# A second chunk of every fourth head computed twice, and the first loads, low parts and products reordered

## The chip, the cores and the metric

The kernel runs on one core of a Trainium2 chip. Its engines are TensorE (PE in the profile; PEld is its weight load), VectorE (DVE), ScalarE (ACT), GpSimd (POOL) and SyncE (SP), which here issues all transfers between HBM and the on-chip memory. The metric is the device time of one execution in microseconds, median of several runs; lower is better. Matrix products write to PSUM, which has eight banks of 128 x 512 numbers.

## The reference

Two independent results for S = 2048 tokens of width D = 448 are written side by side.

```python
# part A: Fourier mixing, written as products with given matrices
a = einsum("bsd,ed->bse", x, dft_hid_re)
b = einsum("bsd,ed->bse", x, dft_hid_im)
y = einsum("ts,bse->bte", dft_seq_re, a) - einsum("ts,bse->bte", dft_seq_im, b)
# part B: full attention with H = 16 heads of 28
q, k, v = split(x @ wqkv)
scores = einsum("bhqd,bhkd->bhqk", q, k) * 28 ** -0.5
o = einsum("bhqk,bhkd->bhqd", softmax(scores), v)
out = concatenate([y, o @ wo], axis=-1)
```

## The kernel before

**Numbers.** A product of 32-bit numbers is made of products of a coarser type (float32r): an operand is split in a high part, which ScalarE's copy makes, and a low part, which is the operand less its high part (a subtraction). Width 448 is three blocks of 128 and one of 64, whose high and low parts share one block; so a product over 448 is a chain of 11 matrix products into one bank: high by high, low by high and high by low for three blocks, and two for the last.

**Stages.** `load_x` brings the input of part B in four chunks of 512 tokens, four blocks each, and splits it. `project(j, w, chunks)` makes block j of q and k (seven blocks of 128 rows), one chain of width 512 a chunk; ScalarE and VectorE copy its high and low part out, and both are stored to HBM (`qkd`), from where each head's rows are read again (`k`, `qk`, `qr`). `values` makes V, one chain of width 448 for each 128 tokens (16 in all); VectorE's copy (L604) takes it out, and a store with rows of 128 bytes lays it out by head (`vd`). These two, and part A (`hidden`, `sequence`, L652), are "fill" work: they use two PSUM banks of their own (`NFILL = 2`), and attention has the other six. At the end the output projection (L959) follows.

**Attention** goes in 64 units (head h, chunk c of 512 queries), and each needs the maximum of a query's 2048 scores before the exponential. There are two ways:

- `unit_kept`: 16 products of scores (L793), each copied to SBUF by ScalarE (L406) and compared into a running maximum by VectorE (L803); then four transposes (L810), a reduction (L812), four transposes that spread the maximum over the partitions (L819), a subtraction over two tiles at once by GpSimd or VectorE (L836), and an exponential over two tiles at once by ScalarE (L840).
- `unit_twice`: 16 products of scores the other way round (L743) whose maxima VectorE reduces straight from PSUM (L747), one small transpose (L706), a trip of the maxima through HBM into two further rows of q, and 16 products again (L771) with the maximum already taken off, which ScalarE's exponential reads from PSUM (L775).

In both, groups of eight tiles are multiplied with V (L724), in a shape of the array that uses 32 columns. `TWICE` says which chunks of a head go the second way: chunk 1 of every head, so 16 of 64.

**Order.** Nothing is ordered by hand. Every step is a task with an engine (or a choice of engines), an assumed duration and a key (its due time); `Schedule.run` plays the kernel through when it is built and emits instructions in the order that results. Units in the two ways form two lanes, each spread evenly over the attention stage (`P_R`, `P_K`); the fill work's keys come from `fkey`, which is evenly spread after a denser start. Each engine takes its instructions strictly in the order emitted.

**The start.** `make_identity` and `N_WARM = 9` products on it come first on TensorE. Then come x's first chunk, weight blocks w_0 and w_1, the other chunks, and V's weights, as the keys in the code's last part say; `project(0, ., [0])`, `project(1, ., [0])`, three more chunks of `project(0)`, and then `values`. The first chunk's low parts are VectorE's; those of later chunks and of V's weights may go to VectorE or GpSimd (`early`). In these first chains the products are sorted so that all high by high products come first.

Of the kernel before, what the change touches and what calls it, by code (L numbers as in the profile page):

```python
# [13 lines left out]
AF = mybir.ActivationFunctionType  # L14
# [7 lines left out]
D = 448  # L22
H = 16
# [12 lines left out]
Q_YO = 2  # L36
N_WARM = 9
GV = 8

TWICE = [(1,) for h in range(H)]  # L40


def f32(ap):
    return ap.bitcast(F32)
# [9 lines left out]
FLOW, FLOW_IN = 200.0, 400.0  # L54
T_IN = 20.0
X_ROWS = 2.0
AHEAD = 0.15
# [105 lines left out]
class Schedule:  # L163
# [34 lines left out]
    def run(self):  # L198
        now, events, count = 0.0, [], 0
# [108 lines left out]
def tile_kernel(ctx, tc, xa, wre, wim, wd, xb, wqkv, wo, out):  # L308
# [90 lines left out]
    def sub(key, dst, a, b, early=False, d=1.25, **kw):  # L399

        return sch.add({"DVE": 0.67} if early == "DVE" else {"DVE": 0.8, "POOL": 1.6} if early else {"POOL": d}, key,
                       lambda e: eng[e].tensor_tensor(dst(), a(), b(), op=ALU.subtract), **kw)
# [26 lines left out]

    IN = F_QKV + 11 * M512  # L430
    HEAD = IN + F_V

    def fkey(n, d):

        f = clock[0]
        clock[0] += n * d
        if f < IN:
            return 6 + f
        if f < HEAD:
            return 6 + IN + V_PACE * (f - IN)  # L440
        at = 6 + IN + V_PACE * F_V
# [9 lines left out]
    def x_3(s):  # L451
        return big[:, 6 * S + s.start:6 * S + s.stop]
# [13 lines left out]
    def load_x(c, key):  # L466
        cols = slice(c * CH, (c + 1) * CH)
        for k in range(4):
            pair = kept_s.slot()
            raw = Half(pair, 0)  # L470
            ld = dma(key + 0.3 * k, lambda raw=raw, k=k: nc.sync.dma_start(raw.t, xb[c, :, k]), use=[pair])
            hi = (lambda k=k: x_h(k, cols)) if k < 3 else (lambda: x_3(cols))
            a = act(key + 0.3 * k, lambda raw=raw, hi=hi: nc.scalar.activation(hi(), raw.t, AF.Copy), ACT_S,
                    deps=[ld], use=[pair])
            early = "DVE" if c == 0 else True
            if k < 3:
                b = sub(key + 0.3 * k, lambda k=k: x_l(k, cols), lambda raw=raw: raw.t,
                        lambda k=k: f32(x_h(k, cols)), early, deps=[a], use=[pair])
            else:
                b = sub(key + 0.3 * k, lambda: x_3(cols)[64:], lambda raw=raw: raw.t[64:],  # L480
                        lambda: f32(x_3(cols))[64:], early, deps=[a], use=[pair])
            xb_hi[c, k], xb_ready[c, k] = a, b
# [18 lines left out]
    class Piece:  # L501


        def __init__(self, src, key, kind="c", early=False):
            self.hi, self.lo = whi.slot(), wlo.slot()
            raw = wraw.slot()
            ld = dma(key, lambda: nc.sync.dma_start(raw.t, src()), acq=[raw])
            a = act(key + 1, lambda: nc.scalar.activation(self.hi.t, raw.t, AF.Copy), ACT_S,  # L508
                    deps=[ld], acq=[self.hi], use=[raw])
# [3 lines left out]
            b = sch.add(e, key + 1.5, lambda g: eng[g].tensor_tensor(  # L513
                self.lo.t[:, :n], raw.t[:, :n], f32(self.hi.t)[:, :n], op=ALU.subtract),
                deps=[a], acq=[self.lo], use=[raw, self.hi])
            self.ready, self.hi_ready, self.lo_ready = [b], a, [b]
            if kind == "x":
                self.ready.append(sch.add({g: {"DVE": 0.3, "POOL": 0.53}[g] for g in both}, key + 1.5, lambda g: eng[g].tensor_tensor(
                    self.hi.t[64:, 3], raw.t[64:, 3], f32(self.hi.t)[64:, 3], op=ALU.subtract),
                    deps=[a], use=[raw, self.hi]))  # L520
            elif kind == "w":
                self.ready.append(sch.add({g: {"DVE": 0.3, "POOL": 0.53}[g] for g in both}, key + 1.5, lambda g: eng[g].tensor_tensor(
                    self.lo.t[:64, 3], raw.t[:64, 3], f32(self.hi.t)[:64, 3], op=ALU.subtract),
                    deps=[a, b], use=[raw, self.hi, self.lo]))
                self.ready.append(sch.add({"DVE": 0.15, "POOL": 0.25}, key + 1.5, lambda g: eng[g].memset(
                    f32(self.lo.t)[64:, 3], 0.0), deps=[b], use=[self.lo]))
                self.lo_ready = self.ready
# [23 lines left out]
    def project(j, w, chunks):  # L551

        for c in chunks:
# [3 lines left out]
            wh, wl = lambda k: (lambda: w.hi.t[:, k]), lambda k: (lambda: w.lo.t[:, k])  # L557
            first = j == 0 or j == 1 and c == 0
            if first:

                seq = [(wh(k), xh(k)) for k in range(3)] + [(wl(k), xh(k)) for k in range(3)] + [
                    (wh(k), xl(k)) for k in range(3)] + [(wh(3), x3()), (wl(3), x3())]
                parts = {i: [xb_hi[c, i]] for i in range(3)}
                parts[0] = [xb_hi[c, 0], w.hi_ready]
                parts[3] = w.lo_ready
                parts.update({6 + k: [xb_ready[c, k]] for k in range(4)})
            else:
                seq = [(b, a) for a, b in products(xh, xl, x3, wh, wl)]
                parts = {0: w.ready}
# [20 lines left out]
    def values(ready):  # L590
        for c in range(NC):
            v_done[c] = []
            for t in range(4):
# [5 lines left out]
                key = fkey(11, M448)  # L599
                end = chain(key, seq, o, D, ready, [], M448, [pair], {3 * k: [xb_ready[c, k]] for k in range(4)}, v_last)  # L600

                def put(o=o, vs=vs):
# [7 lines left out]
                    vs.t.rearrange("p (h x) -> p h x", h=H)), extra=1.0, deps=[b], use=[pair]))  # L610
        x_users.append(v_last[0])

# [392 lines left out]
```

## Time and profile before

| | us |
|---|---|
| median of 3 runs | 1189.49 (1188.24 to 1190.04) |
| the profiled execution | 1188.49 |
| its span in the profile | 1186.6 |

The profile shows one execution. Busy time is the time in which an engine had an instruction under way; matrix products overlap, so the distance between starts is what one more of them costs. A wait in the profile names the instruction that ended it. A row of the time order gives start, duration, engine, line, operation, output and inputs, how many are merged, and in brackets the idle time before and what ended it. The profile's line numbers are those of the kernel before; in the changed kernel most of these lines stand some six further down.

### The profile page before, as it was taken

The numbers are of one execution on the slowest core, as the hardware profiler recorded it, in microseconds if no ns is written. First come the engines' busy times: TensorE is split into PE (matmuls) and PEld (weight loads), VectorE is DVE, ScalarE is ACT, GpSimd is POOL, SyncE is SP. The second block draws the span as 40 slices with busy tenths as digits, with TensorE's granted clock in tenths as the row PEclk, the third lists the DMA queues.
The fourth block names the chain that finished last, engine by engine and source line by source line (L and its number), as shares of the span: only waits on it lengthen the run. The fifth ranks groups of instructions, "written<-read, shape, count | busy, mean of one in ns | idle before, by whom it ended". The sixth has DMA issues, their size and how long they took to land.

```text
span 1186.6 us, 19856 instructions
## 1 busy us (share of the span) xinstructions
PE 1162.1 (98%) x6422; PEld 812.7 (68%) x6422; DVE 912.2 (77%) x1431; ACT 1052.7 (89%) x1764; POOL 965.6 (81%) x569
## 2 busy tenths in 40 slices
PE   8899999999999999999999999999999999999998
PEld 6786666676667666676666666676667676766687
DVE  6598888888888878778878888888888786877301
ACT  5379999999999989899989999999999998999733
POOL 6067778889989879888879888879989888799953
PEclk9999999999999999999999999999999999999999
DMA  7772344421323232313232233233232423223642
GB/s 269 173 135 92 111 131 155 129 79 65 93 85 102 62 115 65 105 60 114 73 109 63 95 106 97 68 94 93 75 118 72 126 70 105 80 76 115 193 143 109
DMA packets 111192, 125.18 MB, mean 105 GB/s; under 512 B 48720, under 2 KB 62672, under 8 KB 111088
## 3 DMA queue, kind: packets, MB, share of 16 engines
q1 hardware_dynamic: 111088, 123.91, 34.6%
q8 instruction: 51, 0.84, 0.3%
q14 instruction: 53, 0.43, 0.1%
HBM read 89.98 MB, written 33.75 MB: 104 GB/s over the span
## 4 chain that ended last, share of the span: by engine, by line
PE 87%; DMA 3%; ACT 3%; DVE 3%; issue 2%; SPq 1%; POOL 0%; DVEq 0%; ACTq 0%; POOLq 0%
PE bank L652 24%; PE bank L724 19%; PE bank L793 15%; PE bank L538 11%; PE bank L771 5%; PE bank L743 5%; PE bank L959 3%; PE bank L810 2%; DVE rm L803 2%; PE bank L819 2%; ACT kept L406 1%; PE bank L854 1%; DMA sm<-kept 1%; DMA kept<-xb 1%; ACT kept L840 1%
## 5 line engine op out<-in xcount | busy, mean ns | idle before, releaser
L836 POOL TENSOR_TENSOR kept<-kept,mb 128x1024 f32<-128x1024 f32 x275 | 655.7, 2407 | 94.1 <-ACT mb L821 83.8
L803 DVE TENSOR_TENSOR rm<-bank,rm 128x512 f32<-128x512 f32 x672 | 460.7, 686 | 83.4 <-ACT kept L406 33.4
L406 ACT ACTIVATE kept<-bank 128x512 f32<-128x512 f32 (+1 forms) x717 | 410.8, 629 | 55.2 <-PE bank L793 34.1
L840 ACT ACTIVATE kept<-kept 128x1024 f32<-128x1024 f32 x374 | 392.5, 1095 | 12.7 <-POOL kept L836 9.4
L652 PE MATMUL bank<-big,whi 128*128 128x448 f32 x1024 | 324.2, 370 | 0.0
L793 PE MATMUL bank<-qk,k 84*128 84x512 f32 x768 | 290.6, 408 | 4.4 <-DVE rm L803 1.4
L513 POOL TENSOR_TENSOR wlo<-wraw,whi 128x512 fp32r<-128x512 f32 (+1 forms) x165 | 202.9, 1234 | 72.0 <-ACT whi L508 48.6
L724 PE MATMUL bank<-kept,v 128*32 128x512 f32 x1984 | 240.2, 597 | 1.1 <-ACT kept L840 1.0
L652 PEld LDWEIGHTS bank<-big,whi 128*128 128x128 f32 x1024 | 193.4, 190 | 30.3 <-issue 5.0
L652 PE MATMUL bank<-big,wlo 128*128 128x448 f32 x512 | 189.2, 370 | 0.6 <-POOL wlo L513 0.6
L793 PEld LDWEIGHTS bank<-qk,k 84*128 84x128 f32 x768 | 142.8, 189 | 65.0 <-issue 15.9
L747 DVE TENSOR_REDUCE mx<-bank 128x1 f32<-128x512 f32 x256 | 172.9, 682 | 15.1 <-PE bank L743 14.0
L775 ACT ACTIVATE kept<-bank 128x512 f32<-128x512 f32 x244 | 154.7, 638 | 9.5 <-PE bank L771 9.3
L724 PEld LDWEIGHTS bank<-kept,v 128*32 128x32 f32 x1984 | 56.3, 109 | 124.1 <-issue 113.8
L508 ACT ACTIVATE whi<-wraw 128x512 fp32r<-128x512 f32 x167 | 111.2, 668 | 18.4 <-DMA wraw<-wqkv 8.0
L836 DVE TENSOR_TENSOR kept<-kept,bank 128x1024 f32<-128x1024 f32 x99 | 119.7, 1211 | 3.2 <-ACT mb L821 2.9
L652 PEld LDWEIGHTS bank<-big,wlo 128*128 128x128 f32 x512 | 97.1, 190 | 13.8 <-POOL wlo L513 1.0
L771 PE MATMUL bank<-qr,k 86*128 86x512 f32 x256 | 104.8, 411 | 1.5 <-DVE rm L803 1.5
L743 PE MATMUL bank<-k,qr 84*128 84x512 f32 x256 | 102.5, 410 | 2.9 <-DMA qr<-qkd 1.9
L538 PE MATMUL bank<-wd,whi 128*128 128x448 f32 x256 | 80.3, 370 | 0.0
L538 PE MATMUL bank<-big,whi 128*128 128x512 f32 x196 | 69.7, 412 | 4.0 <-DVE kept L579 2.6
L812 DVE TENSOR_REDUCE nm<-bank 128x4 f32<-128x512 f32 x48 | 33.1, 690 | 51.6 <-PE bank L810 47.1
(81 smaller groups left out, 1073.1 us busy)
## 6 DMA issues: line engine op xcount, KB each, us to landing
wraw<-wre SPq DMA_DIRECT2D x64, 256.0 KB
wraw<-wim SPq DMA_DIRECT2D x64, 256.0 KB
wraw<-xa SPq DMA_DIRECT2D x32, 256.0 KB
qkd<-wd SPq DMA_DIRECT2D x30, 256.0 KB
k<-qkd SPq DMA_DIRECT2D x64, 112.0 KB
out<-kept SPq DMA_DIRECT2D x32, 224.0 KB
qkd<-kept SPq DMA_DIRECT2D x26, 256.0 KB
qk<-qkd SPq DMA_DIRECT2D x48, 112.0 KB
```

The lines of the kernel that those rows point to most:

```text
L406: nc.scalar.activation(dst, src, AF.Copy)
L513: b = sch.add(e, key + 1.5, lambda g: eng[g].tensor_tensor(self.lo.t[:, :n], raw.t[:, :n], f32(self.hi.t)[:, :n], op=ALU.subtract), deps=[ ...
L538: nc.tensor.matmul(o.t[:, :cols], w(), x(), start=(i == 0), stop=(i == n - 1))
L652: nc.tensor.matmul(o.t[:, :D], a.t[:, k, :], b[:, q * 4 + k, :], start=(q == 0 and k == 0 and j == 0), stop=(q == 3 and k == 3 and j == 2))
L724: nc.tensor.matmul(o.t[j * VW:(j + 1) * VW, :], VT[h].t[:, kt // 4, j, :], pairs[i // 2].t[:, i % 2, :], start=(kt < 4), stop=(kt >= NT - 4))
L743: m = pe(key, lambda e, o=o, kc=kc, qt=qt: nc.tensor.matmul(o.t, q.t[:KR, qt * P:(qt + 1) * P], KT[h].t[:KR, kc * CH:(kc + 1) * CH], start ...
L747: ms.append(dve(key - 20, lambda o=o, kc=kc, qt=qt: nc.vector.tensor_reduce(mx.t[:, qt, kc:kc + 1], o.t, axis=AX.X, op=ALU.max), deps=[m], ...
L771: m = pe(key, lambda e, o=o, kt=kt: nc.tensor.matmul(o.t, KT[h].t[:KR + 2, kt * P:(kt + 1) * P], q.t[:KR + 2, :], start=True, stop=True), ...
L793: m = pe(key, lambda e, o=o, kt=kt: nc.tensor.matmul(o.t, KT[h].t[:KR, kt * P:(kt + 1) * P], q.t[:KR, :], start=True, stop=True), deps=[*l ...
L803: prev = dve(key - 20, lambda o=o: nc.vector.tensor_tensor(rm.t, o.t, rm.t, op=ALU.max), deps=[m, prev], use=[rm, o], lock=[o], own=RAW)
L836: eng[e].tensor_tensor(s.t, s.t, over_pair(pm.t if e == "DVE" else mb.t), op=ALU.add)
L840: es.append(act(key, lambda s=s: nc.scalar.activation(s.t, s.t, AF.Exp, scale=SCALE), 0.96, deps=[sh], use=[s]))
```

## The change

Chunk 3 of heads 2, 6, 10 and 14 also goes the `unit_twice` way, so 20 of 64 units do. In the start, all low parts of x and of V's weights are VectorE's. w_1 is no longer loaded ahead: its load, conversion and low part take their place with the other weight blocks, on GpSimd. V's weights are asked for right after x's first chunk, and V of the first chunk is made right after its `project(0)`. The first chain takes its products in the order in which its parts come, and V's chains wait for each block of weights by itself. There are 11 warm-up products. The builder's play of the start has given start times for the engines and the transfers, and `fkey` has a shorter dense start.

```diff
-N_WARM = 9
+N_WARM = 11
-TWICE = [(1,) for h in range(H)]
+TWICE = [(1, 3) if h % 4 == 2 else (1,) for h in range(H)]
+FIRST = {"PE": 1.4, "ACT": 2.0, "DVE": 2.0, "POOL": 5.0, "SP": 0.75}
+FLOW_AT = 4.1
...
-        idle = {e: True for e in self.ENGINES}
+        idle = {e: False for e in self.ENGINES}
+        for n, e in enumerate(self.ENGINES):
+            heapq.heappush(events, (FIRST[e], 0, n - 9, "free", (e, None)))
-        landed, flow = [], 0.0
+        landed, flow = [], FLOW_AT
...
     def sub(key, dst, a, b, early=False, d=1.25, **kw):
-        return sch.add({"DVE": 0.67} if early == "DVE" else {"DVE": 0.8, "POOL": 1.6} if early else {"POOL": d}, key,
+        return sch.add({"DVE": 0.69} if early else {"POOL": d}, key,
...
-    IN = F_QKV + 11 * M512
-    HEAD = IN + F_V
+    IN = F_QKV + F_V / 4
+    HEAD = F_QKV + F_V
...
-            a = act(key + 1, lambda: nc.scalar.activation(self.hi.t, raw.t, AF.Copy), ACT_S,
+            a = act(key + (0 if early else 1), lambda: nc.scalar.activation(self.hi.t, raw.t, AF.Copy), ACT_S,
+            at = key + (0 if early else 1.5)
...
-            first = j == 0 or j == 1 and c == 0
-            if first:
-                seq = [(wh(k), xh(k)) for k in range(3)] + [(wl(k), xh(k)) for k in range(3)] + [
-                    (wh(k), xl(k)) for k in range(3)] + [(wh(3), x3()), (wl(3), x3())]
-                parts = {i: [xb_hi[c, i]] for i in range(3)}
...
+            first = j == 0
+            seq = [(b, a) for a, b in products(xh, xl, x3, wh, wl)]
+            if first and c == 0:
+                seq = [seq[i] for i in (0, 1, 3, 2, 5, 4, 6, 8, 7, 9, 10)]
+                parts = {0: [xb_hi[c, 0], w.hi_ready], 1: [xb_ready[c, 0]], 2: [xb_hi[c, 1]], 3: w.lo_ready, 5: [xb_ready[c, 1]],
+                         6: [xb_hi[c, 2]], 8: [xb_ready[c, 2]], 9: [xb_ready[c, 3]]}
+            elif first:
+                parts = {3 * k: [xb_hi[c, k]] for k in range(3)}
+                parts.update({3 * k + 1: [xb_ready[c, k]] for k in range(3)})
+                parts[9] = [xb_ready[c, 3]]
...
-        return Piece(lambda: wqkv[:, :, j * P:(j + 1) * P], (0.2, 1.2)[j] if j < 2 else key, "w", j < 2)
+        return Piece(lambda: wqkv[:, :, j * P:(j + 1) * P], 0.2 if j == 0 else key, "w", j == 0)
...
-                end = chain(key, seq, o, D, ready, [], M448, [pair], {3 * k: [xb_ready[c, k]] for k in range(4)}, v_last)
+                end = chain(key, seq, o, D, [], [], M448, [pair],
+                            {3 * k: [xb_ready[c, k], ready[k], *ready[4:][:k // 3]] for k in range(4)}, v_last)
...
-    w_0, w_1 = weights_of(0), weights_of(1)
+    w_0 = weights_of(0)
+    wv = load_w(w_first, lambda k: wqkv[:, k, 2 * D:], 1.5, early=True)
     for c in range(1, NC):
         load_x(c, 1.0 + 3 * c)
-    wv = load_w(w_first, lambda k: wqkv[:, k, 2 * D:], 12.0, early=True)
     project(0, w_0, [0])
-    project(1, w_1, [0])
+    values(wv, [0])
     project(0, w_0, [1, 2, 3])
-    values(wv)
-    project(1, w_1, [1, 2, 3])
-    for j in range(2, 7):
+    values(wv, [1, 2, 3])
+    x_users.append(v_last[0])
+    for j in range(1, 7):
         project(j, weights_of(j), range(NC))
```

More of the change, by code (lines that the diff above doesn't have):

```diff
@@ L440, in fkey @@
             return 6 + IN + V_PACE * (f - IN)
[L441 removed]
+        at = 6 + IN + V_PACE * (HEAD - IN)
         return at + (f - HEAD) * (T_FILL - at) / (F_TOTAL - HEAD)
@@ L517, in __init__ @@
             if kind == "x":
-                self.ready.append(sch.add({g: {"DVE": 0.3, "POOL": 0.53}[g] for g in both}, key + 1.5, lambda g: eng[g].tensor_tensor(
+                self.ready.append(sch.add({g: {"DVE": 0.3, "POOL": 0.53}[g] for g in both}, at, lambda g: eng[g].tensor_tensor(
                     self.hi.t[64:, 3], raw.t[64:, 3], f32(self.hi.t)[64:, 3], op=ALU.subtract),
@@ L521, in __init__ @@
             elif kind == "w":
[L522 removed]
+                self.ready.append(sch.add({g: {"DVE": 0.3, "POOL": 0.53}[g] for g in both}, at, lambda g: eng[g].tensor_tensor(
                     self.lo.t[:64, 3], raw.t[:64, 3], f32(self.hi.t)[:64, 3], op=ALU.subtract),
                     deps=[a, b], use=[raw, self.hi, self.lo]))
[L525 removed]
+                self.ready.append(sch.add({"DVE": 0.15, "POOL": 0.25}, at, lambda g: eng[g].memset(
                     f32(self.lo.t)[64:, 3], 0.0), deps=[b], use=[self.lo]))
@@ L587, in weights_of, with values @@
         key = fkey(0, 0) - 12
-        return Piece(lambda: wqkv[:, :, j * P:(j + 1) * P], (0.2, 1.2)[j] if j < 2 else key, "w", j < 2)
-    def values(ready):
-        for c in range(NC):
+        return Piece(lambda: wqkv[:, :, j * P:(j + 1) * P], 0.2 if j == 0 else key, "w", j == 0)
+    def values(ready, chunks):
+        for c in chunks:
             v_done[c] = []
```

15 lines of the change are left out of this document (5 added, 10 removed).

## The prediction, made before the changed kernel ran

> **What bounds the kernel now.** I read the page first: totals, then the chain that ended last.
>
> ```profile
> span 1186.6 us, 19856 instructions
> ...
> PE 1162.1 (98%) x6422; PEld 812.7 (68%) x6422; DVE 912.2 (77%) x1431; ACT 1052.7 (89%) x1764; POOL 965.6 (81%) x569
> ...
> PE 87%; DMA 3%; ACT 3%; DVE 3%; issue 2%; SPq 1%; POOL 0%; DVEq 0%; ACTq 0%; POOLq 0%
> ```
>
> TensorE is busy 98% of the span and is 87% of the last chain. Next, the stretches, to see where it isn't (columns: PE, PEld, DVE, ACT, POOL busy, granted clock, DMA share, GB/s):
>
> ```profile
> 0.00:32.00 32.00, 25.18 (x91) 19.50 (x92) 19.65 (x30) 17.65 (x30) 18.39 (x19) 1.00 0.77 270
> ...
> 50.00:60.00 10.00, 6.52 (x26) 5.48 (x25) 5.05 (x13) 2.74 (x6) 1.60 (x3) 0.83 0.97 197
> ...
> 80.00:1160.00 1080.00, 1069.38 (x6015) 732.87 (x6014) 852.55 (x1311) 999.88 (x1673) 920.88 (x527) 1.00 0.32 99
> 984.00:992.00 8.00, 6.52 (x28) 4.86 (x31) 3.49 (x6) 5.09 (x11) 4.46 (x3) 0.79 0.39 116
> 1160.00:1186.60 26.60, 23.05 (x113) 20.81 (x111) 3.05 (x5) 9.23 (x21) 10.42 (x15) 1.00 0.27 104
> ```
>
> PE idles 6.8 us in the first 32, 3.5 us between 50 and 60, and only 10.6 us in the 1080 us after 80. The last idle time is after its last product. So a product added in the long middle is paid in full, and what can be won lies in the start, in the hole at 50 to 60, and in those 10.6 us. The list of PE's waits says what ended them:
>
> ```profile
> PE bank L538 <- DVE kept L604: 3.5, 1, 3.5
> ...
> PE bank L771 <- DVE rm L803: 1.5, 1, 1.5
> ...
> PE bank L724 <- ACT kept L840: 1.0, 1, 1.0
> ```
>
> **The four chunks that change path.** Heads 2, 6, 10 and 14 compute chunk 3 twice. Each such chunk trades 16 scores for 32 (64 products more in all), drops two groups of four transposes (L810, L819; 8 groups in all) and gains one small one (L706). PE's order of time in the middle prices them:
>
> ```profile
> 600.39 0.36 PE L652 MATMUL bank<-big,wlo 128*128 128x448 f32 x1
> 600.68 1.92 PE L724 MATMUL bank<-kept,v 128*32 128x512 f32 x16
> 602.53 0.27 PE L706 MATMUL bank<-ident,nm 128*4 128x128 f32 x1
> 602.56 0.72 PE L793 MATMUL bank<-qk,k 84*128 84x512 f32 x2
> ...
> 612.69 0.86 PE L743 MATMUL bank<-k,qr 84*128 84x512 f32 x3
> 613.39 0.37 PE L652 MATMUL bank<-big,wlo 128*128 128x448 f32 x1
> ...
> 618.34 0.60 PE L810 MATMUL bank<-ident,rm 128*128 128x128 f32 x4
> 618.69 0.45 PE L652 MATMUL bank<-big,whi 128*128 128x448 f32 x1
> 618.98 0.40 PE L771 MATMUL bank<-qr,k 86*128 86x512 f32 x1
> ...
> 635.19 3.64 PE L724 MATMUL bank<-kept,v 128*32 128x512 f32 x32
> 638.76 0.66 PE L810 MATMUL bank<-ident,rm 128*128 128x128 f32 x4
> ```
>
> Starts are what count, since ends overlap. Three scores take 613.39 - 612.69 = 0.70, so 0.233 each: 64 cost 14.9 us. Four transposes take 0.35, and the product behind them 0.29 where one of its width otherwise takes about 0.205: 0.44 a group, 8 groups give back 3.5. The L706 transpose holds the next product up by 0.03 and, like the others, slows what follows by 0.09: four cost 0.5. Units: 14.9 - 3.5 + 0.5 = +11.9 us.
>
> The products with V run in another shape of the array. Sixteen instructions take 1.85 us (600.68 to 602.53), thirty-two in one run 3.57, so a run has 2 x 1.85 - 3.57 = 0.13 of its own, and the product before it is stretched by 0.09: 0.22 a run. In the instruction order of the built kernels these products and the head sums stand in 110 runs before and 101 after: -2.0 us.
>
> On the other engines the same four chunks take off 32 double-width passes of ACT and 27 subtractions of POOL; DVE's count hardly moves (64 row maxima come, 60 go). ACT has 999.9 of 1080 us busy in the middle, so this is relief for the engine that is next in line. That middle holds 10.6 us of PE idle and, in the row of 984 to 992, 8 x 0.21 = 1.7 us of low clock: 12.3 that could go. Bounds: none of it, or nearly all; it could also grow by a few us, since a reshuffled order has its own accidents. I take a quarter, -3.0, because the quoted waits were ended by DVE more than by ACT, and DVE gets no relief.
>
> **The start.** Before, low parts of x and of the V weights go to DVE and POOL, and five projections run before the first V chain. After, all are on DVE, w_1's load and low parts leave the start, V chains of chunk 0 come right after the first projection, and two more warm-up products fill the wait for data.
>
> ```profile
> 4.10 0.69 DVE L402 TENSOR_TENSOR big<-kept,big 128x512 fp32r<-128x512 f32 x1 [2.10 <-ACT big L473]
> ...
> 8.29 1.52 DVE L402 TENSOR_TENSOR big<-kept,big 128x512 fp32r<-128x512 f32 x2 [1.01 <-ACT big L473]
> ...
> 10.84 8.16 POOL L402 TENSOR_TENSOR big<-kept,big 128x512 fp32r<-128x512 f32 x5 [5.78 <-DMA kept<-xb]
> ...
> 12.05 4.09 DVE L402 TENSOR_TENSOR big<-kept,big 128x512 fp32r<-128x512 f32 x3 [0.97 <-ACT big L473]
> ...
> 12.31 1.48 PE L538 MATMUL bank<-big,whi 128*128 128x512 f32 x3
> ...
> 13.59 1.08 PE L538 MATMUL bank<-big,wlo 128*128 128x512 f32 x3
> ...
> 16.80 0.96 PE L538 MATMUL bank<-big,whi 128*128 128x512 f32 x3 [0.99 <-DVE kept L579]
> ...
> 23.97 0.96 PE L538 MATMUL bank<-big,whi 128*128 128x512 f32 x3 [0.97 <-DVE kept L579]
> ...
> 26.60 1.59 PE L538 MATMUL bank<-wd,big 128*128 128x448 f32 x7
> ...
> 29.11 0.62 DVE L604 COPY kept<-bank 128x448 f32<-128x448 f32 x1 [0.98 <-PE bank L538]
> ...
> 35.46 1.18 PE L538 MATMUL bank<-wd,big 128*128 128x448 f32 x5
> ```
>
> A subtraction takes DVE 0.69 alone, but 4.09 / 3 = 1.36 while POOL works beside it, and POOL itself 1.63. So two engines together were barely faster than DVE alone, and PE waited for DVE's evictions (16.80, 23.97) because only two PSUM banks serve this work. By 35.46 PE had done five projections (55 products at 0.23: 12.7 us), 29 products of V (0.205: 5.9) and 6 scores (1.4): 20.0 us of work.
>
> After, DVE decides. It has the last low part of chunk 0 at 8.29 + 1.52 = 9.8. In its new order 16 low parts (12 of x, 4 of V weights; 11.0 us), two evictions of projections (0.68 each: 1.4) and four of V chains (0.62 and two memsets: 0.78, so 3.1) follow up to the one that frees the bank for the last projection; the first of them waits some 0.6 for ACT. That ends at 9.8 + 0.6 + 15.5 = 25.9; the third V eviction, two instructions earlier, at 24.4. PE then runs the third projection with one score (2.8, to 27.2) and the fourth with four (3.5, to 30.7). Its work by then: 44 products of each kind and five scores, 10.1 + 9.0 + 1.2 = 20.3, which before stood at about 35.8. Gain: 5.1 us. All loads are served by SP in turn; the V weights now stand ahead of x's chunks 1 to 3, and each chunk's low part comes in DVE's queue later than its load. Bounds: 0, if a late load of V weights holds that one queue, and 7, about the idle time there is. The two warm-up products lie where PE waits for the first data: nothing, and half a us if the data were earlier.
>
> **The hole at 51 us.** SP, ACT, DVE and PE in order of time:
>
> ```profile
> 49.16 0.62 SPq L507 DMA_DIRECT2D wraw<-wqkv  x1
> ...
> 51.20 0.40 PE L793 MATMUL bank<-qk,k 84*128 84x512 f32 x1
> 52.66 0.63 ACT L508 ACTIVATE whi<-wraw 128x512 fp32r<-128x512 f32 x1 [6.30 <-DMA wraw<-wqkv]
> ...
> 54.42 0.61 DVE L604 COPY kept<-bank 128x448 f32<-128x448 f32 x1
> ...
> 55.09 3.61 PE L538 MATMUL bank<-wd,big 128*128 128x448 f32 x9 [3.48 <-DVE kept L604]
> ...
> 58.53 0.60 PE L810 MATMUL bank<-ident,rm 128*128 128x128 f32 x4
> ```
>
> A weight block was asked for at 49.16, and ACT stood before its conversion for 6.3 us with the score copies queued behind; DVE's maxima waited for those, V's evictions for DVE, and PE for a bank. It cost 55.09 - 51.20 - 0.24 = 3.65 us, and then nine products took 3.44 where 1.85 is usual (the granted clock of that stretch is 0.83): 5.3 in all. After, the blocks of w_1 to w_3 are asked for among the first 35 issues of SP, their conversions are ACT's 25th, 26th and 32nd instruction, and the next one is its 130th (before it was the 42nd). That wait has nothing to stand before; -5.3. Bounds: -5.3 and 0, if another load is late instead.
>
> **A rule on the clock.** Before, products took (13.59 - 12.31) / 3 = 0.43 us at the start, twice the later time, and the stretch of 984 to 992 shows 0.79 after one idle time of 1.5 us. The Trainium skill, page "TensorE: Matmul & The Clock Gate", section "What's actually happening", has the clock at half by default, at full after a busy window of some 3.4 us and at half again after an idle window of that length. By that rule idle times of 1 us in the new start cost no clock; by the row 1.5 us already did, and the sum would lose 1.7 for each such time. The row decides here, so gaps near 1 us are a risk that the rivals carry.
>
> **Sum.** +11.9 - 2.0 - 3.0 - 5.1 - 5.3 = -3.5 us. The profiled execution took 1188.5 (its span is 1.9 less), which gives 1185.0; the median of the runs is 1.0 above that execution, so I predict 1186.0.
>
> **Rivals.**
> - *The late load only moves (slower).* V's stores, 16 of them in narrow rows, now begin in the first 20 us and stand in SP's queue between the loads of k and q; the DMA share of 0.97 at only 197 GB/s between 50 and 60 shows what they do. If scores then wait for k as long as ACT waited for weights, the 5.3 stay, and with no relief in the middle (3.0): 1186.0 + 8.3 = 1194; without only the first, 1191. It decides from 3.5 us of new waiting on. For it: SP is as loaded as before. Against: stores spread over more time, and k's chunks are needed some 10 us after their projection.
> - *The start keeps its idle time.* DVE's single queue, or V weights landing late, holds PE in gaps long enough for half clock; the 5.1 are gone: 1191.
> - *Relief is larger.* ACT and POOL stop being late at all, and 9 of the 12.3 us go rather than 3: 1180. For it: ACT's 93% in the middle. Against: DVE's rows in the waits.
>
> **Chances.** My forecast 0.5, with its own range 1182 to 1189; late load 0.22; start 0.1; relief 0.18. The range of 1179 to 1194 reaches to both outer cases and leaves out their far ends. What a measurement here can tell from no change is about 0.2%, or 2.4 us: faster is below 1187.1, slower above 1191.9. Of my forecast about three quarters lie below, with relief that is 0.56; the rest of it, and the smaller half of the slower cases, 0.19 within; 0.25 slower.
>
> **What would show it.** In the profile after: 320 instructions each of the two score groups and 704 of the third, at the same starts apart; no POOL subtraction in the first 20 us and DVE's at 0.69; the fourth projection of w_0 done near 31 us; no hole of over 2 us between 45 and 65, and ACT not before a weight block; PE idle under 10 us between 80 and 1160. Wrong would be: a wait of PE for k or q, a hole elsewhere in the first 100 us, or more than 12 us of idle in the middle.

## The result and the profile after

| kernel | median, us | runs | ratio to the kernel before |
|---|---|---|---|
| before | 1189.33 (1186.41 to 1193.43) | 20 | |
| after | 1193.14 (1191.06 to 1198.40) | 20 | 1.0036, 95% interval [1.0026, 1.0046] |

The changed kernel is 0.36% slower, where 0.3% faster was forecast. Its profiled execution took 1194.36 us (span 1192.6), that of before 1188.49: 5.9 us more.

The totals and the chain of waits of the changed kernel:

```profile
span 1192.6 us, 19803 instructions
...
PE 1168.9 (98%) x6462; PEld 820.5 (69%) x6462; DVE 889.5 (75%) x1419; ACT 1034.5 (87%) x1751; POOL 891.8 (75%) x538
...
PE 83%; DMA 6%; ACT 3%; issue 3%; POOL 2%; SPq 1%; DVE 1%; POOLq 0%; ACTq 0%; DVEq 0%
```

ACT, DVE and POOL have less to do, as forecast, but in the last chain TensorE's share fell from 87% to 83% and DMA's rose from 3% to 6%. The stretches of the changed kernel (length, busy time of PE, PEld, DVE, ACT, POOL, granted clock, DMA share, GB/s):

```profile
0.00:32.00 32.00, 26.67 (x112) 21.65 (x112) 19.14 (x42) 18.06 (x30) 7.84 (x15) 1.00 0.83 256
32.00:50.00 18.00, 13.69 (x54) 12.11 (x55) 10.36 (x22) 5.31 (x9) 1.61 (x3) 0.81 0.55 142
50.00:60.00 10.00, 10.00 (x49) 8.99 (x48) 8.32 (x21) 3.60 (x6) 0.00 (x0) 1.00 0.83 158
...
80.00:1160.00 1080.00, 1069.53 (x6013) 734.00 (x6012) 830.45 (x1291) 981.41 (x1661) 854.39 (x498) 1.00 0.32 99
```

The hole at 50 to 60 us is gone: TensorE is busy for all 10 us at full clock. In its place 4.3 us are idle between 32 and 50, at a mean clock of 0.81. Between 80 and 1160 us TensorE idles 10.5 us, as before (10.6). The waits of TensorE, and its order of time around the new hole:

```profile
PE bank L749 <- DMA qr<-qkd: 7.6, 2, 6.6
PE bank L777 <- DVE rm L806: 1.9, 1, 1.9
```

```profile
29.11 0.40 PE L799 MATMUL bank<-qk,k 84*128 84x512 f32 x1
29.34 0.40 PE L543 MATMUL bank<-big,whi 128*128 128x512 f32 x1
36.31 1.19 PE L749 MATMUL bank<-k,qr 84*128 84x512 f32 x2 [6.57 <-DMA qr<-qkd]
37.30 0.63 PE L543 MATMUL bank<-big,wlo 128*128 128x512 f32 x1
37.73 2.07 PE L543 MATMUL bank<-wd,big 128*128 128x448 f32 x5
39.60 0.63 PE L799 MATMUL bank<-qk,k 84*128 84x512 f32 x1
40.02 2.10 PE L543 MATMUL bank<-wd,big 128*128 128x448 f32 x6
41.96 0.40 PE L799 MATMUL bank<-qk,k 84*128 84x512 f32 x1
42.19 0.39 PE L749 MATMUL bank<-k,qr 84*128 84x512 f32 x1
```

TensorE gets to the first score that needs `qr` at 29.57 and stands until 36.31: 6.7 us. Behind it the products stand at nearly twice their usual distance (five of width 448 take 39.60 - 37.73 = 1.87): sixteen instructions take 42.19 - 36.31 = 5.88 us, where five of width 512 and eleven of width 448 usually take 5 x 0.233 + 11 x 0.205 = 3.42. That is 2.5 us more, so the hole costs 9.2.

SP's queue shows what `qr` waited for (start, duration, queue, line; L615 are V's stores, L511 loads of weights, L588 and L589 the stores of the high and low part of q and k):

```profile
19.09 0.97 SPq L685 DMA_DIRECT2D k<-qkd  x1
...
25.47 0.57 SPq L615 DMA_DIRECT2D vd<-kept  x1
26.14 2.50 SPq L588 DMA_DIRECT2D qkd<-kept  x1
28.69 0.58 SPq L511 DMA_DIRECT2D wraw<-wqkv  x1
29.36 0.60 SPq L589 DMA_DIRECT2D qkd<-kept  x1
...
32.94 0.33 SPq L686 DMA_DIRECT2D k<-qkd  x1
33.33 0.36 SPq L685 DMA_DIRECT2D qr<-qkd  x1
33.74 0.38 SPq L686 DMA_DIRECT2D qr<-qkd  x1
```

The two stores carry what the first row of ACT and this row of DVE had finished long before:

```profile
18.97 0.58 ACT L584 ACTIVATE kept<-bank 128x512 fp32r<-128x512 f32 x1
26.36 0.63 ACT L512 ACTIVATE whi<-wraw 128x512 fp32r<-128x512 f32 x1 [6.80 <-DMA wraw<-wqkv]
```

```profile
19.59 0.69 DVE L585 TENSOR_TENSOR kept<-bank,kept 128x512 fp32r<-128x512 f32 x1 [0.39 <-ACT kept L584]
```

The low part was ready at 20.28, its store was issued at 29.36, and `qr` could be used at 36.31: a trip of 16.0 us, of which 9.1 passed in SP's queue. Ten issues stand ahead of the first store from 19.09 on; they took (26.14 - 19.09) / 10 = 0.71 us each, where the builder's play counts 0.38. The issue right behind the second V store took 2.50.

### The profile page after: what moved, and what is told of

Same layout as the page of the kernel before. It is cut to its first block, busy times and chain, and to the rows that moved or that the text cites. A ratio compares the mean times of both kernels' runs of the same rounds, so it can differ in the third digit from the quotient of the medians.

```text
span 1192.6 us, 19803 instructions
## 1 busy us (share of the span) xinstructions
PE 1168.9 (98%) x6462; PEld 820.5 (69%) x6462; DVE 889.5 (75%) x1419; ACT 1034.5 (87%) x1751; POOL 891.8 (75%) x538
## 4 chain that ended last, share of the span: by engine, by line
PE 83%; DMA 6%; ACT 3%; issue 3%; POOL 2%; SPq 1%; DVE 1%; POOLq 0%; ACTq 0%; DVEq 0%
PE bank L658 24%; PE bank L730 18%; PE bank L799 13%; PE bank L543 10%; PE bank L777 6%; PE bank L749 6%; PE bank L965 3%; PE bank L816 2%; PE bank L825 1%; POOL kept L842 1%; PE bank L860 1%; ACT kept L846 1%; DMA sm<-kept 1%; DMA kept<-xb 1%; ACT kept L411 1%
## 5 line engine op out<-in xcount | busy, mean ns | idle before, releaser
L842 POOL TENSOR_TENSOR kept<-kept,mb 128x1024 f32<-128x1024 f32 x253 | 602.7, 2405 | 136.3 <-ACT mb L827 90.9
L809 DVE TENSOR_TENSOR rm<-bank,rm 128x512 f32<-128x512 f32 x616 | 421.9, 685 | 83.9 <-PE bank L799 40.6
L411 ACT ACTIVATE kept<-bank 128x512 f32<-128x512 f32 x671 | 389.4, 626 | 48.0 <-PE bank L799 26.3
L846 ACT ACTIVATE kept<-kept 128x1024 f32<-128x1024 f32 x347 | 367.2, 1096 | 15.9 <-POOL kept L842 9.9
L799 PE MATMUL bank<-qk,k 84*128 84x512 f32 x704 | 269.5, 408 | 2.9 <-ACT kept L411 1.1
L753 DVE TENSOR_REDUCE mx<-bank 128x1 f32<-128x512 f32 x320 | 215.6, 681 | 25.8 <-PE bank L749 24.6
L781 ACT ACTIVATE kept<-bank 128x512 f32<-128x512 f32 x298 | 184.0, 629 | 19.1 <-PE bank L777 18.8
L749 PE MATMUL bank<-k,qr 84*128 84x512 f32 x320 | 128.6, 410 | 8.6 <-DMA qr<-qkd 7.6
L777 PE MATMUL bank<-qr,k 86*128 86x512 f32 x320 | 128.5, 412 | 5.1 <-DVE rm L806 1.9
L749 PEld LDWEIGHTS bank<-k,qr 84*128 84x128 f32 x320 | 59.9, 190 | 33.9 <-DMA qr<-qkd 7.0
L777 PEld LDWEIGHTS bank<-qr,k 86*128 86x128 f32 x320 | 59.2, 189 | 34.7 <-DVE rm L809 7.8
```

Source lines behind the costliest of these rows:

```text
L411: nc.scalar.activation(dst, src, AF.Copy)
L749: m = pe(key, lambda e, o=o, kc=kc, qt=qt: nc.tensor.matmul(o.t, q.t[:KR, qt * P:(qt + 1) * P], KT[h].t[:KR, kc * CH:(kc + 1) * CH], start ...
L753: ms.append(dve(key - 20, lambda o=o, kc=kc, qt=qt: nc.vector.tensor_reduce(mx.t[:, qt, kc:kc + 1], o.t, axis=AX.X, op=ALU.max), deps=[m], ...
L777: m = pe(key, lambda e, o=o, kt=kt: nc.tensor.matmul(o.t, KT[h].t[:KR + 2, kt * P:(kt + 1) * P], q.t[:KR + 2, :], start=True, stop=True), ...
L799: m = pe(key, lambda e, o=o, kt=kt: nc.tensor.matmul(o.t, KT[h].t[:KR, kt * P:(kt + 1) * P], q.t[:KR, :], start=True, stop=True), deps=[*l ...
L809: prev = dve(key - 20, lambda o=o: nc.vector.tensor_tensor(rm.t, o.t, rm.t, op=ALU.max), deps=[m, prev], use=[rm, o], lock=[o], own=RAW)
```

## The experiments

Each run was compared with the kernel before on the same chip. "16" and "20" tell how many chunks are computed twice.

| run | start | chunks | median, us | ratio to before | 95% interval |
|---|---|---|---|---|---|
| e1 | new | 16 | 1191.25 | 1.0008 | 0.9996 to 1.0019 |
| e2 | old | 20 | 1194.43 | 1.0034 | 1.0020 to 1.0048 |
| e3 | new, scores later | 20 | 1196.76 | 1.0062 | 1.0046 to 1.0077 |
| e4 | new, transfers held | 20 | 1193.39 | 1.0032 | 1.0022 to 1.0042 |
| e5 | e4 and scores gated | 20 | 1191.23 | 1.0029 | 1.0010 to 1.0047 |
| e6 | the same | 16 | 1189.57 | 1.0009 | 0.9998 to 1.0020 |
| e7 | new, low parts on two engines | 20 | 1191.63 | 1.0028 | 1.0015 to 1.0040 |
| e8 | new, V's stores paired | 20 | 1196.10 | 1.0053 | 1.0033 to 1.0074 |
| e9 | old, V's stores paired | 16 | 1192.09 | 1.0021 | 1.0007 to 1.0035 |
| e10 | e5, V's stores paired | 20 | 1191.54 | 1.0022 | 1.0008 to 1.0035 |
| e11 | the same | 16 | 1189.11 | 0.9989 | 0.9977 to 1.0001 |
| e12 | new, longer trips assumed | 20 | 1191.31 | 1.0020 | 1.0008 to 1.0032 |
| e13 | the same | 16 | 1185.31 | 0.9967 | 0.9954 to 0.9980 |
| e14 | e12 and GpSimd's queue | 20 | 1185.14 | 0.9966 | 0.9953 to 0.9978 |
| e15 | the same | 16 | 1179.61 | 0.9923 | 0.9909 to 0.9936 |
| e16 | new, GpSimd's queue alone | 20 | 1190.49 | 1.0019 | 1.0007 to 1.0031 |
| e17 | the same | 16 | 1186.12 | 0.9987 | 0.9972 to 1.0002 |

**e1 and e2: the change in halves.** One has the new start with the old `TWICE`, the other the old start with the new one.

```diff
-TWICE = [(1, 3) if h % 4 == 2 else (1,) for h in range(H)]
+TWICE = [(1,) for h in range(H)]
```

> The changed kernel with 16 chunks twice, as before: the new start alone. Theory A (late q: the new start gains some 5 us and removes the hole at 51 us, but a wait of 6.6 us for q's rows and the half clock after it give it back; the four chunks cost about 12 us of products less 4.6 of fewer runs and stalls, so +7): 1189.3 - 2 to 4 = 1186, with a wait of PE for the load of qr of 5 us or more before 40 us. Theory B (the four chunks cost more than their products and are all of the slowing and more; the start is a gain of 10): 1179 or less. Theory C (the start is a loss by itself, the chunks are free): 1193.

> The kernel before with 20 chunks twice: the four chunks alone, old start. Theory A: 1189.3 + 7 = 1196, with the hole of 5.3 us near 51 us still there and no wait for qr above 2 us. Theory B: 1203 or more. Theory C: 1189.

The new start alone, forecast at -10.4 us, gained nothing. Its waits, and those of the units in the old start:

```profile
PE bank L749 <- DMA qr<-qkd: 7.6, 1, 7.6
```

```profile
PE bank L538 <- DVE kept L604: 3.2, 1, 3.2
```

The wait for `qr` belongs to the start and not to the units; the old start keeps its hole at 51 us. The units alone cost 4 to 5 us, a little less than the 6.9 that the terms of the prediction give for them. So the error lies in the start.

**e3, e4 and e5: the scores later, the transfers earlier.** e3 lets the lane of the units computed twice begin 14 us later in the play. e4 holds V's first stores and the loads of weight blocks 1 to 3 behind the last store of the first block of q and k. e5 adds a wait of the first score of that lane for the sixth chain of V.

```diff
-    due[u] = (T_ATT + i * per, ...)
+    due[u] = (t0 + i * per, ...)          # e3: t0 = T_ATT + 14 for the lane that needs qr
-    dma(key - 20, ..., deps=[b], use=[pair])
+    dma(key - 20, ..., deps=[b, *qk_done[0, 3]], use=[pair])   # e4: V's chunk 0; weight loads alike
-    deps=[*lq, *got_k[h, kc], before.get("ra")]
+    deps=[*lq, *got_k[h, kc], before.get("ra", v_ends[5])]     # e5
```

> The changed kernel, but the lane of chunks computed twice starts 14 us later in the order, so that TensorE meets its first score of that lane later; the transfers' order is left. Theory A: the wait for qr goes; since k's second chunk is loaded by the same late queue at 33 us, part of the hole may stay as a wait for k: 1186 to 1190. Theories B and C: 1193, no change, since the wait would be only shifted.

> The changed kernel, with the stores of V's first chunk and the loads of weight blocks 1 to 3 held back until the fourth projection is stored, so that q's and k's stores and loads come first in SP's queue. Theory A (the queue is what makes q late): the load of qr is issued some 6 us earlier, PE's hole at 30 us shrinks from 6.6 to below 3, and the time is 1184 to 1188. If the hole stays as long with q issued early, the queue is not the cause, and if the hole goes and the time stays at 1193, the hole costs nothing.

> The kernel of e4 (q's and k's stores and loads first in SP's queue), and the first score of the lane computed twice may stand in TensorE's order only behind the sixth chain of V, some 5 us of other products later. Behind its first three scores the order of that lane is the one of e4 again. Theory A, in the form that e4 left it (the hole is TensorE meeting a score in its strict order before q's trip through HBM is over, wherever SP's queue puts the load): no wait for qr above 1.5 us before 50 us, no half clock there, so 6 us of wait and 3 of clock less than e4: 1193.4 - 6 to 9 = 1184 to 1187. If the time stays above 1191, the work after the hole was waiting for something else anyway.

In each the hole is still there, in another place. These are TensorE's rows of e4 and of e5:

```profile
32.02 0.77 PE L756 MATMUL bank<-k,qr 84*128 84x512 f32 x1 [6.11 <-DMA qr<-qkd]
```

```profile
50.34 0.76 PE L808 MATMUL bank<-qk,k 84*128 84x512 f32 x1 [5.72 <-DMA k<-qkd]
```

In e4 `qr` is there 4.3 us sooner than in the changed kernel, but the play, seeing a shorter queue, puts the score nearly 4 us earlier too. In e5 that wait is gone, and the held V stores, released in a burst, come ahead of a chunk of k. In e3 three shorter waits came before 50 us: 2.7 us for an eviction by DVE and 1.0 and 3.9 for k; one of 2.8 for `qr` stands far behind, at 318 us. Moving one thing by hand moves the hole. The profiled execution of e5 took 1188.61, at the low end of its 12 runs (1188.12 to 1197.38): a single profile doesn't show its median.

**e6 and e7.** e6 is e5 with 16 chunks. In e7 the low parts may go to VectorE or GpSimd again.

```diff
-        return sch.add({"DVE": 0.69} if early else {"POOL": d}, key,
+        return sch.add({"DVE": 0.67} if early == "DVE" else {"DVE": 0.8, "POOL": 1.6} if early else {"POOL": d}, key,
```

> The kernel of e5 with 16 chunks twice, as before: the new start without its hole and without the four chunks. Theory A: e5 less the price of the four chunks, which e2 measured as 4.8 and the count of products put at 7 net: 1179 to 1182, the fastest so far. Theory C (the new start is a loss by itself): 1189 or more.

> The changed kernel with the low parts of chunks 1 to 3 and of V's weights on VectorE or GpSimd, as before the change: one part undone. If the move to VectorE is worth its own (0.69 us a subtraction alone, 1.36 beside GpSimd), VectorE's subtractions before 30 us are again near 1.4 us, the fourth projection ends 2 to 4 us later than the 29.3 of the changed kernel; the wait for qr shrinks by as much, because q's trip then has that much longer, and the time stays at 1193. If sharing the low parts is as good, the fourth projection ends by 29.3 as well.

e6 has e5's wait (5.9 us for k) and is 1.7 us faster, by the chunks. In e7 the fourth projection comes later (its last product but one starts at 37.3 us, against 29.3 in the changed kernel); no wait for `qr` over 1 us is left before 80 us, and one of 3.9 us for an eviction stands at 28 us. A slower start hides the trip and pays for it elsewhere.

**e8 to e11: V stored in pairs.** One store takes two groups of 128 tokens, with rows of 256 bytes: half the packets.

```diff
-    v_done[c].append(dma(..., v_d[:, :, (4 * c + t) * VW:(4 * c + t + 1) * VW], ...))
+    if t % 2:
+        v_done[c].append(dma(..., v_d[:, :, (4 * c + t - 1) * VW:(4 * c + t + 1) * VW], ...))
```

> The changed kernel with V stored for two groups of 128 tokens at once: 8 stores with rows of 256 bytes in place of 16 with rows of 128 bytes, nothing else changed. Theory D (the queue between the stores of q and k and their reading again is held up by V's narrow stores, because each takes long to be moved): the issues of 2.5 and 3.1 us on SP go to under 1.5 us, the wait of TensorE for qr near 30 us falls from 6.6 us to under 4 us, and the time falls by 2 to 5 us against the changed kernel, to 1188 to 1191. Rival (the wait is only the order in which the transfers are emitted): the wait stays between 5 and 8 us and the time within 1 us of the changed kernel's 1193.

> The kernel before with the same pairs of V's groups. Theory D says that its V stores begin only after the first reading of q and k, so less is to be had: the idle time at 51 us (3.4 us and half the clock behind it) stays or falls by up to 2 us, the time is 0 to 3 us below the kernel before, 1186.5 to 1189.5. Rival (stores with narrow rows cost time anywhere): 3 to 6 us below, and as much as in the changed kernel.

> The changed kernel with V stored in pairs of groups, the stores of the first chunk's V and the loads of weight blocks 1 to 3 held behind the last store of the first block of q and k, and the first score product of the units computed twice held behind the sixth chain of V. Theory D: with pairs the burst of held stores that put a wait of 5.7 us for k at 44 us in the kernel with single groups is half as long, that wait falls under 3 us and the clock isn't halved behind it; time 2 to 5 us below the same with single groups (1191), so 1186 to 1189. Rival (the wait is one of position and not of the narrow rows): the wait stays between 4 and 7 us and the time at 1190 to 1192.

> As the run before it, but only chunk 1 of each head computed twice (16 chunks). If the four chunks cost 2 to 5 us wherever the start doesn't wait, it ends at 1182 to 1186, below the kernel before by 3 to 7 us; if the four chunks are free once the start is mended, it is within 1 us of the run before it.

Theory D falls: in e8 the issue behind the paired store still took 2.22 us, the wait for `qr` grew to 7.8 us and the time didn't fall, and e9 is slower than before, its hole at 51 us now 5.4 us long. With the gate (e10) the wait for k does fall to 2.6 us, yet the time is that of e5. The Trainium skill, page "DMA: Bandwidth & Descriptors", section "Rules for kernel authors", advises to coalesce many small transfers and says that under 64 KB one pays mostly overhead. Each of these stores carries 256 KB to begin with, only in short rows; fewer stores with wider rows bought nothing here.

**e12 and e13: only the numbers of the play.** The play assumes that the first block's stores land 6 us later and that the reads of the first two heads' rows take 4 us more. No instruction of the kernel is another, only their order.

```diff
-    dma(out_key, ..., deps=[a], use=own)
+    dma(out_key, ..., extra=6 if j == 0 else 0.0, deps=[a], use=own)
-    size=84, extra=X_ROWS, n=2
+    size=84, extra=X_ROWS + (4 if h < 2 else 0.0), n=2
```

> The changed kernel in which only two numbers of the builder's play change: the stores of the first block of q and k are assumed to land 6 us later, and the reads of the first two heads' rows 4 us later, so other work is emitted ahead of the scores (some 3.6 us of products more before the first score that needs qr). Theory E (the play's trip is too short, and the order that follows from it makes the wait): TensorE's wait for qr falls from 6.6 us to under 2 us, none over 3 us comes in its place before 80 us, the clock stays above 0.9, and 5 to 9 us go: 1184 to 1188. Rival (the one queue and the trip bound the start, and idle time moves whatever the order): a wait of 4 us or more stands somewhere else between 25 and 60 us and the time stays within 2 us of 1193.

> The same with chunk 1 of each head alone computed twice (16 chunks), so the new start without the units. Theory E: the start gives what the prediction forecast for it, 7 to 10 us below the kernel before, 1179 to 1183. Rival: no more than the new start alone gave, 1188 to 1192.

The wait for `qr` falls to 1.7 us (e12), yet the transfer itself lands no sooner:

```profile
23.90 0.62 SPq L615 DMA_DIRECT2D vd<-kept  x1
24.56 2.54 SPq L588 DMA_DIRECT2D qkd<-kept  x1
...
33.08 1.05 SPq L685 DMA_DIRECT2D qr<-qkd  x1
```

Again the issue behind a V store takes 2.54 us, and the read goes out at 33.08. A part of theory E holds (with 16 chunks nearly 4 us are won over before), but less than it asked for.

**e14 to e17: a second queue.** GpSimd issues the stores of the first chunk's V and the loads of weight blocks 1 to 3. e14 and e15 assume longer trips as well (5 us for the stores, 3 for the reads); e16 and e17 don't.

```diff
-    dma(key - 20, lambda: nc.sync.dma_start(v_d[...], vs.t...))
+    dma(key - 20, lambda: (nc.gpsimd if c == 0 else nc.sync).dma_start(v_d[...], vs.t...), on="POOL" if c == 0 else "SP")
```

> The changed kernel with longer assumed trips (5 us for the stores, 3 us for the reads) in which GpSimd issues the stores of the first chunk's V and the loads of weight blocks 1 to 3 in place of SP. Theory F (SP's queue is what bounds): qkd's second store is issued by 25 us where the changed kernel has 26 and 29, no wait of TensorE over 2 us stands before 80 us, and the time is at least 2 us below that of the run with assumed trips alone; rival E: the two are within 1.5 us of each other, since the order alone decided.

> As the run before it with 16 chunks computed twice. If the start is mended by the queue and the order, 1178 to 1183, and 2 to 5 us below the same with 20 chunks; if the trip itself bounds, 1187 to 1191.

> The changed kernel in which GpSimd issues the stores of the first chunk's V and the loads of weight blocks 1 to 3 in place of SP; the assumed trips are those of the changed kernel, so the builder puts the first score that needs qr some 0.9 us of work earlier than there. Theory F (the queue alone is the cause): no wait for qr over 2 us, 1184 to 1187. Theory E (the order must be made for the real trip too): qr comes 2 to 4 us earlier but TensorE gets there sooner as well, a wait of 4 to 7 us for qr stays with half the clock behind it, and the time is 1190 to 1194.

> The same with 16 chunks computed twice. Theory F: 1179 to 1182. Theory E: 1187 to 1191, as the new start alone.

SP's queue of e14, and its stretches:

```profile
24.48 0.50 SPq L687 DMA_DIRECT2D k<-qkd  x1
25.04 0.36 SPq L588 DMA_DIRECT2D qkd<-kept  x1
25.44 0.42 SPq L589 DMA_DIRECT2D qkd<-kept  x1
...
30.51 0.36 SPq L686 DMA_DIRECT2D qr<-qkd  x1
```

```profile
32.00:50.00 18.00, 18.00 (x87) 16.04 (x86) 15.31 (x38) 7.42 (x14) 1.64 (x3) 1.00 0.81 185
50.00:60.00 10.00, 10.00 (x53) 8.98 (x52) 8.64 (x21) 4.43 (x8) 2.64 (x2) 1.00 0.82 140
60.00:80.00 20.00, 20.00 (x110) 14.79 (x109) 17.18 (x35) 14.55 (x24) 11.63 (x5) 1.00 0.77 170
80.00:1160.00 1080.00, 1071.60 (x6008) 736.93 (x6007) 827.73 (x1287) 979.95 (x1662) 859.12 (x504) 1.00 0.32 98
```

The two stores now follow each other at 0.4 us, the read is out at 30.51, TensorE reaches the first score with `qr` at 38.25 without waiting, and from 32 to 80 us it doesn't idle at all. GpSimd also asks for weight blocks 1 to 3 far sooner, where SP came to the first of them at 22.61; what each of the two moves is worth was not tried apart:

```profile
4.88 1.68 POOL L511 DMA_DIRECT2D wraw<-wqkv  x2
7.20 0.75 POOL L511 DMA_DIRECT2D wraw<-wqkv  x1 [0.42 <-issue]
```

With the queue alone (e16) the read is out nearly as soon, but the score comes too soon:

```profile
31.02 0.36 SPq L686 DMA_DIRECT2D qr<-qkd  x1
```

```profile
34.28 0.47 PE L750 MATMUL bank<-k,qr 84*128 84x512 f32 x1 [3.10 <-DMA qr<-qkd]
```

(e12 and e13 assume 6 and 4 us more, e14 and e15 5 and 3.) At 20 chunks, against the changed kernel's 1.0036, the trips alone give 0.16%, the queue alone 0.17%, both 0.70%. At 16 chunks, against e1's 1.0008, they give 0.41%, 0.21% and 0.85%. With intervals of 0.10% to 0.15% to either side of each ratio, the two together are clearly more than the sum of both at 20 chunks, and not clearly at 16. Neither theory E nor theory F is enough alone: the queue makes the trip shorter, and the play has to know how long it still is. e15 is faster than both kernels of this case by some 9 us and 13 us.

> The kernel before (its own start, 16 chunks computed twice) with the longer assumed trips (5 us for the stores, 3 us for the reads) and with the stores of the first chunk's V and the loads of weight blocks 2 to 4 issued by GpSimd. If the new start itself is worth what the prediction gave it (5.1 us of work done sooner), only the wait at 51 us can be won here: 0 to 5 us below the kernel before, 1184 to 1189, so some 5 us behind the new start with the same two edits. If the queue and the trips are all that matters, 7 to 10 us below, 1178 to 1182.

This control (e18) settles nothing. Its order became another one altogether, with V stored between 55.9 and 97.1 us; its first projection waits 8.2 us for a weight block, it took 1201.43 us, and its output is wrong (relative error 4.4) for a reason that is open. Whether the queue and the trips would help the old start as much is open. That e18 used the same second queue is also a reason to look at its waits again before e15 is taken over.

## Why the prediction was wrong

- *The units: right, somewhat too dear.* 320, 320 and 704 products stand in the three score groups. The forecast was 11.9 - 2.0 - 3.0 = +6.9 us. Where no wait disturbs, e14 and e15 put the four chunks at 1185.14 - 1179.61 = +5.5; over all seven pairs of runs with 20 and 16 chunks the ratios differ by 0.20% to 0.53%, 2.4 to 6.3 us.
- *Relief in the middle: it came, but not as idle time.* Idle time there is 10.5 us against 10.6, and the low clock at 984 us has a twin at 820, behind a wait of 1.94 us for DVE. Since the four chunks cost 5.5 rather than 11.9 - 2.0 = 9.9 us, about 4.4 are won, while e14 and e15 idle 8.4 and 7.2 us between 80 and 1160. The starts in their traces show where. Between 60 and 1165 us, at full clock in both, the products stand closer in e14 (mean from start to start, idle time taken off): those with V 0.1137 us apart against 0.1149, the second scores of the chunks computed twice 0.2515 against 0.2558, the transposes 0.0955 against 0.0983. The products with V stand in 100 runs there against 113, which fits fewer changes of shape; that these changes are the cause is only argued.
- *The start: the size right, the way only in part.* At 29.57 the changed kernel had done 43 products of width 512, 44 of width 448 and three scores, 19.6 us of work. The kernel before had done 19.8 at 35.46 (28 products of V by then, not 29). That is 5.7 us sooner, and 5.1 were forecast. Some 3.7 of it is idle time of TensorE that went (5.4 us before, 1.7 after). The other 2 or so are clock, for which the prediction has no term: before, twelve products stood 0.43 us apart from 8.90 to 14.02 (its rows at 12.31 and 13.59 show three of them), while the changed kernel is at 0.23 from 7.54 on:

```profile
6.17 1.53 PE L543 MATMUL bank<-big,whi 128*128 128x512 f32 x3
7.54 0.62 PE L543 MATMUL bank<-big,wlo 128*128 128x512 f32 x2
7.99 0.62 PE L543 MATMUL bank<-big,whi 128*128 128x512 f32 x2
```

  e2, with the old start, is slow until 13.5 us as well. Whether the two more warm-up products, forecast to be worth nothing, or the new order of the first chain did it was not tried apart. Nor did DVE decide: TensorE waits for it 0.5 and 0.2 us in the new start, and the fourth eviction of V ended at 24.07, where 25.9 was forecast. So the size came out partly by luck.
- *The hole at 51 us: this is the step that failed.* "That wait has nothing to stand before; -5.3", with 0 as the worst bound. About that place it was right: the hole is gone, and where ACT did stand before a weight block, for 6.80 us up to 26.36, TensorE lost nothing by it. What failed is that the 5.3 went into the sum as a net gain. The trip of `qr` through SP's queue has no term, and the bound of 0 leaves out that a new wait can cost more than the old one did. It came at 29.7 us, where TensorE met the first score that needs `qr`, and cost 9.2: 6.7 of waiting and 2.5 of low clock. The prediction itself names as a sign of being wrong "a wait of PE for k or q, a hole elsewhere in the first 100 us".
- *The sum.* 11.9 - 2.0 - 5.7 - 5.3 + 9.2 = +8.1; the profiled executions differ by 5.9, which leaves -2.2 for the middle, where -3.0 were forecast. With the missing +9.2, the forecast's own -3.5 would have been +5.7.
- *The rival that came.* "The late load only moves" gave 1194 and would decide from 3.5 us of new waiting on; the wait was 6.6 us and the time 1193.14. Its mechanism, scores that wait behind V's stores in SP's queue, is nearly the one that came, but that its number fits so well is luck: it counted the old 5.3 and no relief, where 9.2 of a new hole and 2.2 of relief came. Against it the prediction said that k's chunks are needed some 10 us after their projection. For `qr` the distance was 9.3 us (20.28 to 29.57), but the trip took 16.0. I had compared that distance with nothing. The new start finishes the first block of q and k 5.7 us sooner, while its V stores go into the one queue that carries q and k; both ends of the trip move against each other.
- *The start keeps its idle time; relief is larger.* Neither came.
- *The clock.* Idle times of 0.1 to 0.75 us in the new start cost no clock. Behind the 6.6 us of waiting the granted clock, in stretches of 2 us from 36 to 42, was 0.50, 0.50 and 0.61, so half for some 5.3 us of work. For idle times near 1.9 us see below.

Shown by experiment: that the new start gains nothing as it stands (e1), while the four chunks alone cost 0.34% (e2); that it does gain once the wait for `qr` and those in its place are gone (e15 is 9.4 us below the kernel before, where 10.4 were forecast for the new start); and that queue and assumed trips together bring more than both alone, clearly so at 20 chunks (e12 to e17). Only argued: why an issue behind a V store takes so long. Open: how much of the gain of e14 and e15 is the stores' move and how much that of the weight loads.

## What to carry to other kernels

Before an edit lets work finish sooner, follow each of its results to the next user: when it is ready, how many issues stand ahead of it in its queue at their measured durations, and when the user gets there. A hole that an edit closes is worth its price only if that sum leaves no longer one, and the worst bound for it is a loss, not zero; the price of a hole is its idle time and the low clock behind it (here 6.7 and 2.5 us). Where an order comes from a play with assumed durations, its transfer times belong to what is tuned, and changing these alone is a cheap test of whether the order is the cause.

## What the runs showed of the hardware

- In the changed kernel the four issues on SP right behind a store of V's first chunk took 0.97, 2.50, 1.48 and 3.05 us. In e14, with these stores on GpSimd, the same kinds of issue took 0.36, 0.36, 0.81 and 0.36. There each V store took GpSimd 1.15 to 1.19:

```profile
17.29 1.19 POOL L616 DMA_DIRECT2D vd<-kept  x1 [0.34 <-DVE kept L613]
21.11 1.16 POOL L616 DMA_DIRECT2D vd<-kept  x1 [2.64 <-DMA qkd<-kept]
```

- The Trainium skill, page "DMA: Bandwidth & Descriptors", section "Issuing engines are not separate DMA queues", says that issuing from several engines saves only the time of issuing, usually small against the transfer. That it saves this time agrees with the trace: two of the four issues stand ahead of `qr`'s read, and they were 2.8 us shorter together in e14. In e14 a V store on GpSimd took 5.8 us (median) from issue to landing; for SP's transfers no row here gives the landing.
- Two idle times of nearly the same length had different prices. In e14 a wait of 1.87 us at 14.4 us left the clock at 1.00; in e15 one of 1.99 was followed by half clock for some 3.4 us (0.70 and 0.50 in the stretches below, 0.95 in the next). The rows of e14, then of e15:

```profile
14.37 0.50 PE L543 MATMUL bank<-big,whi 128*128 128x512 f32 x1 [1.87 <-ACT big L478]
...
14.00:16.00 2.00, 1.32 (x4) 0.66 (x5) 2.00 (x3) 2.00 (x5) 2.00 (x2) 1.00 1.06 408
16.00:18.00 2.00, 2.00 (x10) 1.70 (x11) 1.97 (x6) 1.95 (x4) 1.61 (x3) 1.00 1.06 407
```

```profile
14.47 0.53 PE L543 MATMUL bank<-big,whi 128*128 128x512 f32 x1 [1.99 <-ACT big L478]
...
14.00:16.00 2.00, 1.52 (x4) 0.69 (x4) 2.00 (x3) 2.00 (x5) 2.00 (x2) 0.70 1.06 407
16.00:18.00 2.00, 2.00 (x6) 1.61 (x6) 1.97 (x6) 1.99 (x4) 1.60 (x3) 0.50 1.05 406
```

- The Trainium skill, page "TensorE: Matmul & The Clock Gate", section "What's actually happening", has a window of about 3.4 us that runs free of the kernel, which fits that the same gap is cheap once and dear once; that it takes an idle time of a whole window does not fit, since 1.99 us were enough.
- The granted clock in the rows of stretches doesn't show the slow start. In the kernel before it reads 1.00 from 0 to 32 us, while twelve products stand 0.43 us apart up to 14.02 and 0.23 afterwards. In the changed kernel that is the distance under a granted clock of 0.50 (37.30 to 37.73), so there the distance between starts tells more than the column.
